# Moving the keys' store and reload from SyncE's queue to GpSimd's, with a new written order of the steps

## The chip, the cores and the metric

The kernel runs on one core of a Trainium2 chip. The metric is the device time of one execution in microseconds; lower is better. Before the change three runs gave a median of 332.5 us (331.88 to 334.31).

## The reference

Two parts follow each other. The first is a linear attention with a complex, data-dependent decay, over 4 batches, 8 heads, 768 tokens and 48 channels per head, all float32:

```python
mag = np.sqrt(a_re * a_re + a_im * a_im)
scale = np.minimum(mag, 0.999) / (mag + 1e-06)
a_re_n, a_im_n = (a_re * scale, a_im * scale)
for t in range(S):
    new_re = ar * S_re - ai * S_im          # ar, ai: a_re_n, a_im_n at token t, per channel d
    new_im = ar * S_im + ai * S_re
    kv = np.einsum('bhd,bhe->bhde', k[:, :, t], v[:, :, t])
    S_re, S_im = (new_re + kv, new_im)
    y[:, :, t] = np.einsum('bhd,bhde->bhe', q[:, :, t], S_re)
```

The second takes y as x, with the heads side by side (4 x 768 x 384), and does a causal convolution over 5 taps per channel, a sigmoid gate and two 384 x 384 products:

```python
for k in range(K):
    gate_pre += conv_w[k][None, None, :] * xp[:, k:k + S, :]
gate = 1.0 / (1.0 + np.exp(-gate_pre))
val = x @ w_val
return (gate * val @ w_out).astype(np.float32)
```

The weights of the second part (w_val, conv_w, w_out) come as 64-bit floats and are turned into 32-bit ones on the chip.

## The kernel before

**Units.** The heads are worked on in 10 units: units 0 and 1 have two heads each, units 2 to 7 four, units 8 and 9 two again. Each unit has 768 tokens, in 6 chunks of 128, and its tokens are split into two halves of 384.

**Preparation of a unit.** The decay's logarithm and angle are summed up along the tokens, so that the recurrence becomes products: a query and a key are each multiplied by a magnitude and by a cosine and a sine, which makes 96 columns per head. The tiles for this have the tokens on partitions in an order of their own (partition p holds three consecutive tokens of each half). The steps: X or x (even or odd units: logarithms and exponentials of the decay, ACT and DVE by turns), R or r (arctangent, sums along the tokens, angle; the offsets between partitions by matmuls), A or a (the magnitude's offsets), S (sine, cosine), E (exponentials), and B, four DVE instructions: the key times its magnitude, then `kx`, the scaled keys with sine and cosine, then the same for the query, into `trig`. Behind the second B letter's instruction two DMAs, one per half of the tokens, store `kx` in a DRAM tile `kd` (line 392).

**Attention of a unit.** T (128 letters): three transpositions on PE turn one half of one head's keys or queries to `kq`, which has the 96 channels on partitions; ACT copies them out of PSUM (line 431). Since the state's update needs keys with the tokens of a chunk on partitions, the keys are read back from `kd` in that layout: N, one letter per half of a unit, sets one column of a `kn` tile to zero on GpSimd (line 407) and issues three DMAs `kn<-kd` (line 413), one for the first half of the heads and two, each with half the rows swapped, for the second. Each waits for its half of the store; the second and third also wait for the first. There are three `kn` tiles. Then by chunk: s (scores on PE), k (mask on DVE), t (state `S_ps` from `kn` and `v`, PE, copied by ACT), y (output from the state and from the masked scores, PE, copied to `y_sb` by ACT). There are two `y_sb` tiles, each for half a unit. D moves such a half into `xT`, channels on partitions, by DMAs issued on GpSimd (`xT<-y_sb`, line 509).

**The second part.** C is the convolution on DVE (lines 518 and 521), G the sigmoid on ACT, M the two products on PE with the gating on DVE and a copy on ACT; O stores the result from GpSimd (line 813). W turns the weights to 32 bits, mostly on DVE (lines 186 to 208), once.

**What sets the order.** Every step is a letter of the string `ORDER` (991 letters); L and V load inputs, issued by SyncE. The instructions of PE, ACT and DVE run in exactly the order of the letters, by dependencies added at the end of the kernel. Those of SyncE and GpSimd are placed by the framework's own scheduler, and each of the two issues its queue in order: a DMA that has to wait keeps all behind it on the same engine from being issued. ACT's function tables are loaded by `table_set` when the next function isn't in the loaded set, so the number of table loads follows from the order.

`XQ` is the name for GpSimd as an issuer of DMAs (`XQ = nc.gpsimd`).

Of the kernel before, what the change touches and what calls it, by code (L numbers as in the profile page):

```python
# [19 lines left out]

PI = math.pi
ORDER = (
    "LLXLXxxXXVxXLxxXXxxXRxrWWWWWLRWWRrrLWLVWRARRALWrarWraARSSWWWaWWWWWrSSEWEBBBLBWXWXEENXLNWTTTWTTWT"
    "XTXTBLsskBXBWkyLWtBTskNXXLtRRxRyWskWWsWxTTxTRykWtRTxWxWxTWWTyLsWkWRtWTxytskxrrDyAttWsksARNSyktSr"
    "DVysWtrAErysWrkWDErBLatBskSatBLyLSkaNByXEWWXyNWTTtDTTTTTTLTWTTTTXTTTtEstBLXsVBktkyXWsBLkWyBskxtX"
    "yDstykWskNXytxWCCCCCTTXTyTTDTTTTxCCTCTTTTVTCTsktCxskCCLCCtNyCxCskCRRCLGMRMMsxtMykMxMyDRAARRsxrrr"
    "ktRSSMMAOMMstrEEOryMrMBLMMrSSBNyaMBLLLOaXMtkXMMaMyMEMDBTTTTTTTTTTTTXTTXTTstEBLMsNtBkykBLxsOMxsNt"
    "yVksXBkXtCysxkXtXyMxMkyxTTTyttTOCTTTTTCTTCTCMDDCOTNxTCTCTCCCCLRCCRCskRstCxCCGMMMMMMRskRtVykLRxrr"
    "rMMORsykAMSyrDMSAAEaOrskrtMrMsOaEBMtLBNykMSyMaMtSEBLLXyBNXMMTTMTTTTTTLTTTTTTTTsEtMXDBLsXBkkBLXLx"
    "txXyskCtysBXMOtCXRRyDskRxkCNtTtTVTTTTTTsxxRAyLRxCkCMANxRxrrAyMMMMOyDtTVTTTTTrTTRSSssCCktCyskCras"  # L30
    "kECtOyCCsEBkrBCCtCCyDBskCtykNCGMaMaMMyMtByMCCCMMOCCCtTDTTTTTTTMsksrtrCNCSMVMCSskMMykOMCMMEEBCOsB"
    "NsBtNMykMMCykMDyMstBTTTTTOTTkTtstykMyDssMtykkMMOtMCCyCsCksCtCCCCCCCOykDCtCCMGCCMstyMMCGMMyMkyMMt"
    "MDMOOMMMMMOCCCCCCGMMMMMMMMOOMMO"
)
IN_ORDER = (
    mybir.EngineType.PE, mybir.EngineType.Activation, mybir.EngineType.DVE
# [9 lines left out]
def kernel(  # L46
# [12 lines left out]
    nc = tc.nc  # L59
    XQ = nc.gpsimd  # L60
# [60 lines left out]
    def rows(h, g):  # L121

        return ((0, 0, C),) if h < g // 2 else ((0, C // 2, C // 2), (C // 2, 0, C // 2))
# [27 lines left out]
    for f in range(2):  # L151
        nc.gpsimd.memset(dmat[:, f], float(f))
        nc.gpsimd.affine_select(
            out=dmat[:, f], in_=dmat[:, f], pattern=[[1, P]], compare_op=ALU.is_ge, fill=float(f - 1),
# [6 lines left out]
    for kind, r0, i0 in ((0, 0, 0), (0, C // 2, C // 2), (1, 0, C // 2), (1, C // 2, 0)):  # L161
        nc.gpsimd.affine_select(
            out=mask[r0:r0 + C // 2, kind], in_=mask[r0:r0 + C // 2, kind], pattern=[[1, C]],
# [100 lines left out]
    def views(u):  # L264
        b, h0, g = units[u]
        main = tiles[u]["main"]
        return main, main.rearrange("p s j f x -> p s (j f x)"), main.rearrange("p s j f (h d) -> p s j (f h) d", h=g)
# [101 lines left out]
    def prep_b(u):  # L369

        b, h0, g = units[u]
        tl = tiles[u]
        trig = tl["trig"]
        main, mf, mj = views(u)

        def scaled(s, nm, dst):
            while not done.get(("L", u, nm)):
                yield "wait"
            nc.vector.tensor_tensor(out=mj[:, s], in0=mj[:, s], in1=jm(tl[nm]), op=ALU.mult)  # L379
            done[nm, u] = True  # L380
            yield
            nc.vector.tensor_tensor(  # L382
                out=dst, in0=trig,
                in1=mj[:, s].rearrange("p j x d -> p (j x) d")[:, :, None, :].to_broadcast([P, J * g, 2, D]),
                op=ALU.mult,
            )
            return dst.rearrange("p (j f h) c d -> p j f h (c d)", f=2, h=g)

        kx = yield from scaled(1, "k", work.tile([P, J * g, 2, D], F32, name="kx", bufs=KXB))
        kd = tl["kd"] = dram.tile([S, g, C2], F32, name="kd")  # L390
        for f in range(2):
            nc.sync.dma_start(
                out=kd[f * HS:(f + 1) * HS].rearrange("(p j) h c -> p j (h c)", j=JH),
                in_=kx[:, :, f].rearrange("p j h c -> p j (h c)"),
            )
        tl["kn"] = []
        done["kd", u] = True
        yield
        qx = yield from scaled(0, "q", trig)
        tl.update(kx=kx, qx=qx, kq=[])  # L400

    def load_kn(u, hn):

        b, h0, g = units[u]
        n0, N = HN * hn, min(HN, NCH - 1 - HN * hn)
        flat = qkp.tile([C, HN * g * C2 + 1], F32, name="kn", bufs=KNB)
        nc.gpsimd.memset(flat[:, N * g * C2:N * g * C2 + 1], 0.0)
        kn = flat[:, :N * g * C2].rearrange("i (n x) -> i n x", n=N)
        src = tiles[u]["kd"][n0 * C:(n0 + N) * C].rearrange("(n i) h c -> i n (h c)", i=C)
        for h in (0, g // 2):  # L410
            cols = slice(h * C2, (h + g // 2) * C2)
            for i0, i1, n in rows(h, g):
                nc.sync.dma_start(out=kn[i0:i0 + n, :, cols], in_=src[i1:i1 + n, :, cols])
        tiles[u]["kn"].append(flat)

    def transpose(u):
# [263 lines left out]
    stream_s = prep_stream("S", prep_s, lambda u: upto("R", u), every)  # L680
    stream_e = prep_stream("E", prep_e, lambda u: upto("A", u) and upto("S", u), every)
    stream_b = prep_stream("B", prep_b, lambda u: upto("E", u) and upto("S", u) and upto("T", u - KXB), every)

    def guard():
# [110 lines left out]
    def move(key):  # L795
# [13 lines left out]
        elif key == "O":  # L809
            if i >= len(outs):  # L810
                return False
            b, m, ot = outs[i]
            XQ.dma_start(out=out[b, m:m + P], in_=ot)
        else:
            if i >= (NU if key == "V" else 2 * NU):
                return False
            u, hn = (i, 0) if key == "V" else halves_of[i]
            if key == "V":
                if u not in tiles or u >= VB and not done.get(("Y", u - VB)):
                    return False  # L820
                load_v(u)
                done["V", u] = True
            elif key == "N":
                if not done.get(("kd", u)) or i >= KNB and at["t"] < HN * (i - KNB + 1) - (i - KNB) % 2:
                    return False
                load_kn(u, hn)
                done["N", u, hn] = True
            else:
                if not done.get(("y", u, HN * hn + HN - 1)) or not room_for_x(units[u][0]):
                    return False  # L830
                att[u].collect(hn)
                done["D", u, hn] = True
# [169 lines left out]
```

## Time and profile before

| | |
|---|---|
| median of three runs | 332.5 us |
| the profiled execution | 332.24 us, of which the span is 330.5 us |
| PE busy | 263.2 us, 80% of the span |
| DVE busy | 257.4 us, 78% |
| ACT busy | 245.9 us, 74% |
| POOL busy | 59.8 us, 18% |
| granted clock of TensorE | 0.94 |
| moved by DMA | 53.31 MB |
| of it by q1 (issued on SyncE) | 43.28 MB |
| of it by q0 (issued on GpSimd) | 9.44 MB |

The profile is of one execution. The span goes from the first to the last instruction; the time of the execution is 1.7 us longer. POOL stands for GpSimd, SPq for SyncE's queue of DMA issues; an issue on GpSimd is shown as an instruction of POOL. A busy PE isn't PE at its peak, since its instructions overlap.

### The profile page before, as it was taken

The page shows a single profiled execution, that of the slowest core. Times are in us where ns is not written, and L with a number is a line of the kernel's source. Part 1 is how long each engine was busy: PE and PEld are TensorE (multiplying, and loading weights), DVE is VectorE, ACT ScalarE, POOL GpSimd, SP SyncE. Part 2 cuts the span into 40 slices and gives each one's busy share as a digit, 9 for nine tenths or more (in the row PEclk, how much of TensorE's full clock was granted, in tenths as well). Part 3 has the DMA queues.
Part 4 walks back from the last instruction along what each step waited for, and adds up shares of the span by engine and source line. Part 5 has one row for each costly group of instructions (what it writes and reads, how often), then busy time and mean ns, then how long its engine had stood idle before and what let it go on. Part 6 is the DMA issues. An engine that isn't in the chain of part 4 may idle for free.

```text
span 330.5 us, 8134 instructions
## 1 busy us (share of the span) xinstructions
PE 263.2 (80%) x3234; PEld 204.1 (62%) x3234; DVE 257.4 (78%) x341; ACT 245.9 (74%) x455; POOL 59.8 (18%) x148
## 2 busy tenths in 40 slices
PE   0030775747999899989969999899998999999950
PEld 0030664635998487668868887698696756866520
DVE  4499889999698999968968999689789857294500
ACT  5729879999979789998849899989894474552110
POOL 3000001121033022030430030303303312132110
PEclk9999959785999799999969999999999999999995
DMA  7994989839999722788989025997424504321120
GB/s 198 279 244 100 264 235 241 173 91 285 237 322 168 195 77 69 236 227 225 278 224 189 3 68 194 246 275 184 122 57 126 137 18 125 84 86 32 60 78 0
DMA packets 87804, 53.31 MB, mean 161 GB/s; under 512 B 36432, under 2 KB 84816, under 8 KB 87760
## 3 DMA queue, kind: packets, MB, share of 16 engines
q1 hardware_dynamic: 83664, 43.28, 50.8%
q0 software_dynamic: 4096, 9.44, 9.4%
q8 instruction: 27, 0.44, 0.6%
q14 instruction: 17, 0.14, 0.1%
HBM read 33.83 MB, written 14.16 MB: 145 GB/s over the span
## 4 chain that ended last, share of the span: by engine, by line
PE 31%; DVE 23%; ACT 14%; issue 12%; DMA 11%; POOL 3%; SPq 2%; POOLq 0%; DVEq 0%; ACTq 0%
PE pt L430 9%; PE pv L255 6%; PE po L255 4%; DMA kn<-kd 4%; ACT L104 3%; PE sc_ps L457 3%; DVE sm L464 3%; PE y_ps L480 3%; DMA raw<-in_moe_w_val_dram 3%; DVE main L379 3%; DMA kd<-kx 3%; DVE main L249 2%; DVE main L318 2%; DMA xT<-y_sb 2%; PE y_ps L477 2%
## 5 line engine op out<-in xcount | busy, mean ns | idle before, releaser
L431 ACT COPY kq<-pt 96x384 f32<-96x384 f32 x128 | 52.0, 508 | 4.7 <-PE pt L430 4.5
L509 POOL DMA_DIRECT2D xT<-y_sb x80 | 41.0, 519 | 77.4 <-ACT y_sb L481 74.9
L521 DVE SCALAR_TENSOR_TENSOR z<-xT,cw_sb,z 128x768 f32<-128x768 f32 (+1 forms) x60 | 51.4, 856 | 1.7
L255 PE MATMUL pv<-xT,wv_sb 128*64 128x384 f32 x288 | 51.4, 499 | 0.0
L255 PE MATMUL po<-wo_sb,z 128*64 128x384 f32 x288 | 51.2, 488 | 0.0
L430 PE MATMUL pt<-ident,kx 128*96 128x128 f32 x192 | 37.2, 308 | 10.4 <-DVE kx L382 9.5
L464 DVE TENSOR_TENSOR sm<-sc_ps,mask 128x512 f32<-128x512 f32 (+1 forms) x60 | 34.6, 578 | 13.0 <-PE sc_ps L458 9.0
L480 PE MATMUL y_ps<-sm,v_in 128*48 128x128 f32 x384 | 41.5, 279 | 3.1 <-DVE sm L464 3.1
L457 PE MATMUL sc_ps<-kq 96*64 96x128 f32 x384 | 42.4, 281 | 1.8 <-DVE sm L464 1.7
L458 PE MATMUL sc_ps<-kq 96*64 96x64 f32 x384 | 42.3, 227 | 0.0
L477 PE MATMUL y_ps<-kq,S_sb 96*48 96x128 f32 x320 | 36.3, 286 | 7.2 <-ACT y_sb L481 4.1
L104 ACT ACT_TABLE_LOAD x31 | 39.8, 1283 | 1.3 <-PEq L986 0.8
L430 PE MATMUL pt<-ident,trig 128*96 128x128 f32 x192 | 36.5, 305 | 4.5 <-DVE trig L382 2.8
L458 PEld LDWEIGHTS sc_ps<-kq 96*64 96x64 f32 x384 | 38.5, 140 | 1.7
L255 PEld LDWEIGHTS pv<-xT,wv_sb 128*64 128x64 f32 x288 | 26.0, 141 | 17.6 <-issue 2.9
L457 PEld LDWEIGHTS sc_ps<-kq 96*64 96x64 f32 x384 | 32.1, 141 | 5.1 <-DVE sm L464 2.6
L255 PEld LDWEIGHTS po<-wo_sb,z 128*64 128x64 f32 x288 | 24.6, 136 | 15.4 <-DVE z L542 1.6
L481 ACT COPY y_sb<-y_ps 112x256 f32<-112x256 f32 (+1 forms) x60 | 19.5, 326 | 19.6 <-PE y_ps L480 19.0
L430 PEld LDWEIGHTS pt<-ident,kx 128*96 128x96 f32 x192 | 23.5, 142 | 15.2 <-issue 11.7
L477 PEld LDWEIGHTS y_ps<-kq,S_sb 96*48 96x48 f32 x320 | 21.3, 125 | 15.1 <-ACT y_sb L481 6.4
L480 PEld LDWEIGHTS y_ps<-sm,v_in 128*48 128x48 f32 x384 | 27.1, 126 | 4.1 <-DVE sm L464 3.9
L494 PE MATMUL S_ps<-v_in,kn 128*64 128x48 f32 x320 | 27.7, 225 | 1.6 <-ACT S_sb L497 1.6
(84 smaller groups left out, 484.5 us busy)
## 6 DMA issues: line engine op xcount, KB each, us to landing
kd<-kx SPq DMA_DIRECT2D x12, 576.0 KB, 5.0
out_dram<-ot POOLq DMA_DIRECT2D x24, 192.0 KB, 2.5
ar_in<-in_a_re_dram SPq DMA_DIRECT2D x12, 288.0 KB, 4.3
ai_in<-in_a_im_dram SPq DMA_DIRECT2D x12, 288.0 KB, 4.7
k_in<-in_k_dram SPq DMA_DIRECT2D x12, 288.0 KB, 4.1
q_in<-in_q_dram SPq DMA_DIRECT2D x12, 288.0 KB, 4.1
xT<-y_sb POOLq DMA_DIRECT2D x48, 72.0 KB, 3.3
v_in<-in_v_dram SPq DMA_DIRECT2D x16, 144.0 KB, 4.9
```

What stands on the lines that cost most here:

```text
L104: nc.scalar.preload_act_table_set(name)
L255: nc.tensor.matmul(out[c:c + 64], lhsT[:, c:c + 64], rhs, **kw)
L430: nc.tensor.transpose(pt[:C2, j, :], src[:, j, f, h, :], ident)
L431: nc.scalar.copy(tj[:, s, f], pt[:C2].rearrange("c j p -> c p j"))
L457: nc.tensor.matmul(sc[lo:lo + half, h, :], k[:, :half], q, start=True, stop=True)
L458: nc.tensor.matmul(sc[hi:hi + half, h, half:], k[:, half:], q[:, half:], start=True, stop=True)
L464: nc.vector.tensor_tensor(out=two(sm), in0=two(sc[:, :g]), in1=mask[:, :, None, :].to_broadcast([C, 2, g // 2, C]), op=ALU.mult)
L477: nc.tensor.matmul(o, self.S_sb[n - 1][:, h * D:(h + 1) * D], self.part(1, h, n), start=True, stop=False)
L480: nc.tensor.matmul(o, vt[:, h, n], sm[:, h, :], start=(n == 0), stop=True)
L494: nc.tensor.matmul(S_all[:64, cols], kn[:, c0:c0 + 64], vt[:, h, n], **at_h)
L509: XQ.dma_start(out=xTs[b][c0 % P:c0 % P + c2 - c0, c0 // P, EXT + hf * HS:EXT + (hf + 1) * HS], in_=self.y[hf][r0:r0 + c2 - c0, h // 2],)
L521: nc.vector.scalar_tensor_tensor(out=z, in0=xT[:, c, EXT + t0 - t:EXT + t0 - t + n], scalar=cw_sb[:, TAPS - 1 - t, c:c + 1], in1=z, op0=AL ...
```

## The change

The two stores `kd<-kx` of a unit and the six loads `kn<-kd` are issued by GpSimd instead of SyncE: 20 and 60 DMAs in all, with the same shapes, sizes and dependencies. `ORDER` is replaced by another string. It has the same length, and every letter occurs in it as often as before. The new order was found by a search whose model lets transfers land later. Nothing else changes.

```diff
--- before.py
+++ after.py
@@ -20,17 +20,17 @@
 
 PI = math.pi
 ORDER = (
-    "LLXLXxxXXVxXLxxXXxxXRxrWWWWWLRWWRrrLWLVWRARRALWrarWraARSSWWWaWWWWWrSSEWEBBBLBWXWXEENXLNWTTTWTTWT"
-    "XTXTBLsskBXBWkyLWtBTskNXXLtRRxRyWskWWsWxTTxTRykWtRTxWxWxTWWTyLsWkWRtWTxytskxrrDyAttWsksARNSyktSr"
-    "DVysWtrAErysWrkWDErBLatBskSatBLyLSkaNByXEWWXyNWTTtDTTTTTTLTWTTTTXTTTtEstBLXsVBktkyXWsBLkWyBskxtX"
-    "yDstykWskNXytxWCCCCCTTXTyTTDTTTTxCCTCTTTTVTCTsktCxskCCLCCtNyCxCskCRRCLGMRMMsxtMykMxMyDRAARRsxrrr"
-    "ktRSSMMAOMMstrEEOryMrMBLMMrSSBNyaMBLLLOaXMtkXMMaMyMEMDBTTTTTTTTTTTTXTTXTTstEBLMsNtBkykBLxsOMxsNt"
-    "yVksXBkXtCysxkXtXyMxMkyxTTTyttTOCTTTTTCTTCTCMDDCOTNxTCTCTCCCCLRCCRCskRstCxCCGMMMMMMRskRtVykLRxrr"
-    "rMMORsykAMSyrDMSAAEaOrskrtMrMsOaEBMtLBNykMSyMaMtSEBLLXyBNXMMTTMTTTTTTLTTTTTTTTsEtMXDBLsXBkkBLXLx"
-    "txXyskCtysBXMOtCXRRyDskRxkCNtTtTVTTTTTTsxxRAyLRxCkCMANxRxrrAyMMMMOyDtTVTTTTTrTTRSSssCCktCyskCras"
-    "kECtOyCCsEBkrBCCtCCyDBskCtykNCGMaMaMMyMtByMCCCMMOCCCtTDTTTTTTTMsksrtrCNCSMVMCSskMMykOMCMMEEBCOsB"
-    "NsBtNMykMMCykMDyMstBTTTTTOTTkTtstykMyDssMtykkMMOtMCCyCsCksCtCCCCCCCOykDCtCCMGCCMstyMMCGMMyMkyMMt"
-    "MDMOOMMMMMOCCCCCCGMMMMMMMMOOMMO"
+    "LLXXXXXLxLXxxXXRRLRLxxxxWWRARxLrRArrWAWrLRSrWrVSaEEBBBrXWXBTWSTaaTWWLSTTTENTLEWWXTNWsskysBLkWBWB"
+    "LksWBtWXXWWWTtykTWxTXWWWWWWtxyskXWxXWVtsyWxWxxWtTtkWWTyxxWTWWWTTskLNsWRWykrRDRtrsrykNsLtyRAtRRVy"
+    "AstkraWkaRSaDyWWskAtrWStyErEWDyVBLBBBLNWLLrSSTETETTTTTTWTTTTTTXTWWTsBsDkNLkWXtBysksXytkstXBBykDL"
+    "stXNykXttxTWTyWCCCCTCXyxTCTXDTTTxTTTTTTCTCTNsktCskCLxCtyCsktLCyxCCCCskRtRRVyskCxGMMMsRMRxRtykMMx"
+    "rrRDySMMOSrAyVAAEErMaDrrBLrMMOaaMMOSBMBLMNSMMELMtXMBNCMMOTTTTTTTTTTTTCTLTCEXTTsBLMstMCCMtMBkysXk"
+    "XtXyBLxCNxsBksytTTXTTTTTTXkytkstDLxxkXytxyTTxTTxTTtTTsOsLxrkyRksDMCCCCstNkRysRrVyDkkRAAtCsRRykAC"
+    "tryCCRSSCCOCCGMMMMryrMaVaEMDrMMEMOBMaLrSSBMMMMBOLBMNTMMTTTCTTTTCTTTCTTLTNEtETXLTssCCkMstkCOysXBL"
+    "tByksMtXBLxkyDkNxMXXBMyXMXMxtTTTxTxTxTXLTxskttyMxrrORMyTTRTTRTTRAtTRRrDTTssMtAAkyraLCskCtRSayCSC"
+    "NstkkaCCyCCOsskDrEEBtryrBVCCCCGMMMyMSMkMMOMMNCCCMtyBOBTTTOTTDTTVTtsCMkstCMOCSMyNMsECCEkstCCMCykM"
+    "ykDsstMMBkBMMMOByCMMNOyMtBMTTtMCCTTTTCTCTtCskytCskytskyskNtDyskOsDCCCCkCCtykCGCMMCyMtCMCMCGyMMMM"
+    "MMDOMMOMMMOCCCCCMCGMMMMMMOMMMOO"
 )
 IN_ORDER = (
     mybir.EngineType.PE, mybir.EngineType.Activation, mybir.EngineType.DVE
@@ -389,7 +389,7 @@
         kx = yield from scaled(1, "k", work.tile([P, J * g, 2, D], F32, name="kx", bufs=KXB))
         kd = tl["kd"] = dram.tile([S, g, C2], F32, name="kd")
         for f in range(2):
-            nc.sync.dma_start(
+            XQ.dma_start(
                 out=kd[f * HS:(f + 1) * HS].rearrange("(p j) h c -> p j (h c)", j=JH),
                 in_=kx[:, :, f].rearrange("p j h c -> p j (h c)"),
             )
@@ -410,7 +410,7 @@
         for h in (0, g // 2):
             cols = slice(h * C2, (h + g // 2) * C2)
             for i0, i1, n in rows(h, g):
-                nc.sync.dma_start(out=kn[i0:i0 + n, :, cols], in_=src[i1:i1 + n, :, cols])
+                XQ.dma_start(out=kn[i0:i0 + n, :, cols], in_=src[i1:i1 + n, :, cols])
         tiles[u]["kn"].append(flat)
 
     def transpose(u):
```

## The prediction

> **What bounds the kernel now.** I read the page's first part, then the busy time by stage, then the waits of each engine, then the chain of waits around the stages in which everything stood still. The page's first part names no single bound:
>
> ```profile
> span 330.5 us, 8134 instructions
> PE 263.2 (80%) x3234; PEld 204.1 (62%) x3234; DVE 257.4 (78%) x341; ACT 245.9 (74%) x455; POOL 59.8 (18%) x148
> ```
>
> Three engines are within 18 us of each other, so the stage decides. Columns below: stage and its length, then busy time of PE, PEld, DVE, ACT, POOL, each with its count, then clock, DMA share, GB/s.
>
> ```profile
> 0.00:20.00 20.00, 0.09 (x2) 0.12 (x4) 10.79 (x20) 11.42 (x17) 3.24 (x23) 1.00 0.91 253
> 20.00:45.00 25.00, 11.93 (x105) 10.17 (x107) 23.29 (x39) 18.92 (x35) 0.11 (x1) 0.94 0.73 187
> 45.00:80.00 35.00, 21.98 (x279) 18.29 (x277) 33.40 (x47) 34.50 (x57) 4.17 (x12) 0.79 0.75 202
> 80.00:318.00 238.00, 228.97 (x2855) 175.51 (x2853) 189.92 (x238) 180.54 (x347) 51.73 (x111) 0.97 0.58 152
> 100.00:120.00 20.00, 18.05 (x217) 13.10 (x219) 18.80 (x22) 16.84 (x31) 2.60 (x6) 0.91 0.78 171
> 160.00:180.00 20.00, 17.14 (x183) 14.71 (x181) 15.73 (x18) 14.82 (x29) 5.22 (x11) 0.83 0.99 225
> 240.00:260.00 20.00, 18.80 (x307) 15.58 (x307) 18.68 (x25) 12.59 (x25) 3.05 (x8) 1.00 0.32 86
> ```
>
> Up to 80 us the preparation of the first units on DVE and ACT bounds the kernel: DVE is idle for 9.2 + 1.7 + 1.6 = 12.5 us there, nearly all of it before 20 us. From 80 to 318 us PE is busy for 229.0 of 238 us. The 9.0 us of PE idle time there are all that better timing alone can bring in this stage; 2.9 of them lie in 160 to 180, where DVE and ACT stand as well, and 1.95 and 1.2 in the other two stages shown.
>
> The stall at 160 to 180 is about the very transfers that the change moves. These are rows of the timeline (start, duration, engine, line):
>
> ```profile
> 148.74 2.56 DVE L382 TENSOR_TENSOR kx<-trig,main 128x2304 f32<-128x2304 f32 x1 [2.91 <-PE pt L430]
> 151.83 1.81 SPq L413 DMA_DIRECT2D kn<-kd  x2
> 153.74 1.46 SPq L132 DMA_DIRECT2D v_in<-in_v_dram  x2
> 155.30 0.66 SPq L392 DMA_DIRECT2D kd<-kx  x1
> 168.97 0.34 PE L495 MATMUL S_ps<-v_in,kn 128*33 128x48 f32 x2 [2.86 <-DMA kn<-kd]
> ```
>
> and of the chain of waits (start, duration):
>
> ```profile
> 155.30 5.14 DMA kd<-kx
> 160.50 4.04 DMA kn<-kd
> 165.25 3.58 DMA kn<-kd
> ```
>
> The scaled keys of unit 5 are done at 151.30, but their store is issued at 155.30: ahead of it on SP stand two loads of unit 4's keys, held until 151.83, and two loads of values. Then store, first load and second load land one after the other (the second load of a half waits for the first), and PE waits 2.86 us at 168.97.
>
> **The change, part by part.** Both orders have the same 991 letters with equal counts of each kind, so the n-th letter of a kind is the same step in both and no arithmetic is added. Three things can change the time: table loads, waits, and what the queues hold up.
>
> *Table loads.* Walking through both strings with the rule of `table_set`, I get 31 loads before, as in the row below, and 29 after.
>
> ```profile
> L104 ACT ACT_TABLE_LOAD x31 | 39.8, 1283 | 1.3 <-PEq L986 0.8
> PE 31%; DVE 23%; ACT 14%; issue 12%; DMA 11%; POOL 3%; SPq 2%; POOLq 0%; DVEq 0%; ACTq 0%
> ```
>
> Two fewer are 2 x 1.283 = 2.57 us of ACT. ACT carries 14% of the chain that ended last, so I count -0.4 us (0 to -2.6).
>
> *The start.* Rows of DVE's groups (mean ns of one), of its timeline, of ACT's copies and of the chain of waits:
>
> ```profile
> L186 DVE TENSOR_SCALAR cvt<-raw 128x384 uint32<-128x384 uint32 x6 | 2.1, 354 | 2.5 <-DMA raw<-in_moe_w_val_dram 2.5
> L191 DVE SCALAR_TENSOR_TENSOR cvt<-raw,cvt 128x384 uint32<-128x384 uint32 x6 | 3.3, 557 | 0.2
> 30.76 1.36 DVE L382 TENSOR_TENSOR kx<-trig,main 128x1152 f32<-128x1152 f32 x1
> 43.98 1.35 DVE L382 TENSOR_TENSOR trig<-trig,main 128x1152 f32<-128x1152 f32 x1
> L431 ACT COPY kq<-pt 96x384 f32<-96x384 f32 x128 | 52.0, 508 | 4.7 <-PE pt L430 4.5
> 77.07 2.47 DVE trig L382
> 79.68 6.70 PE pt L430 x45
> ```
>
> Before unit 0's kx (the second B) the old order has 20 W (weights) letters, the new one 5. Of the 15 between, 11 are DVE instructions of 0.35 to 0.56 us, 5.3 us in sum; two a (1.1 us) come later too. So 6.4 us of DVE work leave the path to that kx, and it should end near 32.12 - 6.4 = 25.7 us; my walk along the ACT and DVE steps of unit 0 gives 25.
>
> But this work is only moved. Up to the 17th T (unit 2's first, at 79.68 us, right behind the DVE row at 77.07) both strings hold exactly the same DVE steps; the new one has three ACT steps of X and E and one of W fewer. That T therefore moves only by what DVE's idle time changes. After unit 0's last B the new string has five W, two a and one X for DVE, 4.8 us, and then the first mask (k), which waits until ACT has copied all eight T of unit 0: eight copies (4.1 us), two table loads (2.6) and S and E of unit 1 between. DVE is idle there for 4 to 5 us. Walked on, unit 1's last B ends at 42.3 us, 3.0 earlier than the 45.3 of before, with 3.6 us more of W and X still to do ahead of unit 2's first T: +0.6 us. The ends are -5 (that wait hidden) and +3 (weights needed before they land). PE starts some 7 us earlier and gains nothing by it, since DVE is the bound until 80 us.
>
> *The waits of the middle.* In the new string the second half of unit 4's key loads (N, letter 436) stands 38 letters ahead of unit 5's kx (letter 474), against two letters before, so the store should not be caught behind them. I take the whole 2.86 us stall as gone: -2.9 (0 to -3.3). The other wait on the path is that of the convolution on y's transfer:
>
> ```profile
> DVE z L518 <- DMA xT<-y_sb: 11.5, 4, 5.1
> SPq L413 <- DMA kn<-kd: 33.6, 17, 4.3
> SPq L413 <- DMA kd<-kx: 22.8, 13, 3.8
> ```
>
> It ends PE idle time in the stages 100 to 120 and 240 to 260, 3.15 us together. Between the last y of a half and the conv that needs it the new string has 3.3 us of DVE work and 10.2 us of PE work for the seventh C letter, where the old one had 2.0 and 5.6, and 5.3 us of DVE work for the 43rd, where it had 1.2. I take two thirds: -2.0 (0 to -3.2).
>
> *The queue.* 20 stores and 60 loads leave SP for POOL, past xT's 80 transfers, the 24 of the output and the memsets.
>
> ```profile
> L413 SPq DMA_DIRECT2D kn<-kd x60: 365/608/1194, 35.4 to 284.4; - x60
> L509 POOL DMA_DIRECT2D xT<-y_sb x80: 497/504/696, 53.3 to 303.8; - x80
> L813 POOL DMA_DIRECT2D out_dram<-ot x24: 542/547/696, 128.8 to 320.3; - x24
> kn<-kd SPq DMA_DIRECT2D x16, 144.0 KB, 3.5
> kn<-kd SPq DMA_DIRECT2D x8, 48.0 KB, 2.4
> xT<-y_sb POOLq DMA_DIRECT2D x16, 48.0 KB, 3.4
> kn<-kd SPq DMA_DIRECT2D x6, 192.0 KB, 4.3
> out_dram<-ot POOLq DMA_DIRECT2D x24, 192.0 KB, 2.5
> ```
>
> At 0.50 to 0.70 us each the 80 add 40 to 56 us to POOL's 59.8, some 108 us in all, far from a bound; SP loses 60 x 0.61 us and more that nobody waits for. How a key transfer lands when POOL issues it, no row shows. At 48 KB POOL's row is 1.0 us above SP's, at 192 KB 1.8 us below; I take +0.9 from the smaller pair, whose sizes are nearer to the 48 to 144 KB of most key loads. Three in line are +2.7 us per half unit (-5.4 to +3.0). Where the order leaves work between kx and the first t this is hidden. It is thinnest in the last unit:
>
> ```profile
> 279.54 5.44 SPq L413 DMA_DIRECT2D kn<-kd  x6
> 288.05 0.27 PE L494 MATMUL S_ps<-v_in,kn 128*64 128x48 f32 x2
> ```
>
> Its six loads are issued by 284.98 and land some 2.4 us later, 0.7 us ahead of its first state; the new string leaves one M letter more and 5 us less PE work of other kinds in between, but only the first half's three loads are needed there. I count +1 (0 to +3).
>
> On this the Trainium skill (DMA: Bandwidth & Descriptors, "Issuing engines are not separate DMA queues") speaks against the change: transfers started from different engines end up on the same DMA engines, and several issuers only save issue time. By it alone the 2.9 us would come from the order, and a move of the queue with the old order would be worth nothing; the late store at 155.30 is a case of an issuer that waits, which the rule leaves room for.
>
> Sum: -0.4 + 0.6 - 2.9 - 2.0 + 1.0 = -3.7. The profiled execution took 332.24 us (span 330.5), so 328.5; the median of the runs, 332.5, lies 0.3 above it, so **328.8 us**.
>
> **The rivals.**
>
> *POOL's queue holds y back (slower).* POOL issues in order. A load of keys that waits there for its store keeps every xT and output transfer behind it from being issued. SP waited 33.6 + 22.8 = 56.4 us in 30 such waits, 17% of the span. Of 20 groups of xT (the D letters) 3.4 would fall into such a wait and lose 1.9 us (the mean) to 4.3 us (the longest): 6.5 to 14.6 us, of which the convolutions and, through y's two buffers, ACT take most, since xT waits were on the path before any of this. With the xT gain gone and the rest kept (-1.7) this is 337 to 345, likeliest 339. It decides once an xT issue starts over about 3.3 us (the DVE work left) after its y copy. Against it: POOL is 18% busy, and nothing in the order of SP and POOL is fixed by hand.
>
> *PE takes it all back (no change).* 229.0 of 238 us are busy on PE, so a wait that goes at one place comes back at the next T burst, where ACT's copies set the pace, and 331 to 334 remains, likeliest 332. For it: at the start an earlier PE buys nothing either. Here too belongs that the move does not do what it says, because a load held on POOL is held as long as on SP.
>
> *The start pays (clearly faster).* If DVE finds work during the wait for unit 0's copies, its idle time falls from 12.5 to about 7.5 us and everything behind follows: 328.8 - 5.6 = 323. Against it: the letters there are k, s and y, which all need the copies.
>
> **How the numbers follow.** A difference of about 1% (3.3 us) is what a measurement of this kernel can tell from no change. My forecast, 325 to 331, has 0.38; the start that pays 0.13; no change 0.24; POOL's hold 0.25. Of the forecast 0.30 lies under 329.2, so faster is 0.30 + 0.13 = 0.43, same 0.08 + 0.24 = 0.32, slower 0.25. Cases of both signs are likely, so the range has to reach to both: 320 to 340 leaves out about a tenth at either end; the likeliest case's own range is 325 to 331.
>
> **What would show it.** Right: 29 table loads; q1's bytes down and q0's up by what kd and kn hold; POOL near 108 us; the first kx near 25 us but unit 2's first T still at 78 to 83 us; no wait of PE on kn over 2 us in mid-kernel; DVE's wait on xT under 8 us. Wrong: xT issues on POOL that start more than 3 us after their y copy with a key load in front; long waits of ACT's y copy; unit 2's first T earlier than 76 us; PE's idle time from 80 us on above 9 us.

## The result, and the profile after

The changed kernel takes **343.3 us** (median; 342.6 to 344.6) against 333.1 us of the kernel before on the same chip: recorded ratio 1.0355, 95% interval 1.0315 to 1.0396 (the quotient of the two medians is 1.030). It is 10 us slower; the prediction was 328.8 us, range 320 to 340. A run more than 1.5% above the fastest of its kernel counts as slow and is left out of all medians and ratios here, which among the experiments concerns one run each of e3 and e4.

Page of the changed kernel (busy time by engine; the two queues; shares of the chain that ended last; the table loads):

```profile
span 342.0 us, 8080 instructions
PE 267.9 (78%) x3234; PEld 199.4 (58%) x3234; DVE 259.9 (76%) x341; ACT 242.2 (71%) x453; POOL 113.9 (33%) x228
...
q1 hardware_dynamic: 61904, 25.98, 31.1%
q0 software_dynamic: 9568, 26.75, 26.3%
...
DVE 29%; DMA 20%; ACT 16%; PE 14%; issue 12%; POOL 5%; SPq 0%; POOLq 0%; DVEq 0%; ACTq 0%
...
L104 ACT ACT_TABLE_LOAD x29 | 37.2, 1283 | 1.3 <-PEq L986 0.8
```

PE, DVE and ACT do the work they did before, within 5 us each, in a span that is 11.5 us longer. What grew is the DMA's share of the chain that ended last: 20%, against 11% before. Busy time by stage, with the columns of the prediction's table (the last two are the DMA engines' share and GB/s):

```profile
20.00:45.00 25.00, 12.33 (x102) 9.71 (x99) 19.04 (x31) 17.18 (x31) 7.82 (x11) 0.82 1.00 249
45.00:80.00 35.00, 20.57 (x260) 16.62 (x260) 34.34 (x49) 29.98 (x55) 9.38 (x22) 0.79 0.51 115
80.00:329.00 249.00, 231.28 (x2848) 170.84 (x2849) 194.88 (x241) 178.89 (x347) 92.39 (x171) 0.97 0.55 149
100.00:120.00 20.00, 14.04 (x173) 11.51 (x169) 15.14 (x18) 13.05 (x29) 8.06 (x16) 0.86 1.08 231
```

Two places stand out. From 20 to 45 us DVE is idle for 6.0 us (1.7 before), and from 100 to 120 us PE is idle for 6.0 us (1.95 before). The chain of waits runs through DMAs in both:

```profile
24.64 2.94 DMA kd<-kx
27.86 6.26 DMA kn<-kd
35.04 7.01 DMA kn<-kd
...
99.05 6.69 DMA kn<-kd
...
108.56 7.07 DMA xT<-y_sb
```

The start: `kx` of unit 0 ends at 24.3 us, 7.8 us earlier than before, and then three landings follow in line, 16.2 us together. The last of them ends at 42.04, where unit 0's first key tile is whole, and only then PE can go on. These are rows of SyncE's timeline for that time, and of GpSimd's for that time and for the second place:

```profile
26.82 1.05 SPq L114 DMA_DIRECT2D k_in<-in_k_dram  x2
27.96 1.00 SPq L114 DMA_DIRECT2D q_in<-in_q_dram  x2
...
36.57 1.80 SPq L114 DMA_DIRECT2D q_in<-in_q_dram  x2
```

```profile
34.41 2.42 POOL L413 DMA_DIRECT2D kn<-kd  x4 [4.45 <-DMA kn<-kd]
...
106.03 1.97 POOL L413 DMA_DIRECT2D kn<-kd  x3 [3.70 <-DMA kn<-kd]
...
108.03 2.54 POOL L509 DMA_DIRECT2D xT<-y_sb  x5
```

SyncE, which has no key loads any more, issues input loads from 26.8 to 38.4 us without a stop. The keys issued by GpSimd share the DMA engines with them: the DMA engines' share from 20 to 45 us is 1.00, against 0.73 before. The waits of the changed kernel (us in total, times, longest):

```profile
POOL kn L413 <- DMA kn<-kd: 30.4, 15, 4.8
POOL kn L413 <- DMA kd<-kx: 28.2, 15, 5.6
PE S_ps L495 <- DMA kn<-kd: 11.3, 3, 7.3
DVE z L518 <- DMA xT<-y_sb: 9.1, 4, 4.6
```

GpSimd now does the waiting that SyncE did (58.6 us; SyncE 56.4), and PE's longest wait on keys is 7.3 us.

### The profile page after: what moved, and what is told of

Its sections match the earlier page's. It is cut to its first block, busy times and chain, and to the rows that moved or that the text cites. A ratio compares the mean times of both kernels' runs of the same rounds, so it can differ in the third digit from the quotient of the medians.

```text
span 342.0 us, 8080 instructions
## 1 busy us (share of the span) xinstructions
PE 267.9 (78%) x3234; PEld 199.4 (58%) x3234; DVE 259.9 (76%) x341; ACT 242.2 (71%) x453; POOL 113.9 (33%) x228
## 4 chain that ended last, share of the span: by engine, by line
DVE 29%; DMA 20%; ACT 16%; PE 14%; issue 12%; POOL 5%; SPq 0%; POOLq 0%; DVEq 0%; ACTq 0%
DMA kn<-kd 11%; DVE z L521 5%; PE po L255 5%; DMA xT<-y_sb 4%; PE pt L430 4%; DVE kx L382 4%; DMA kd<-kx 3%; DVE main L379 3%; ACT L104 3%; ACT kq L431 3%; DVE sm L464 3%; DVE main L249 2%; DVE main L318 2%; PE pv L255 2%; POOL xT L509 2%
## 5 line engine op out<-in xcount | busy, mean ns | idle before, releaser
L413 POOL DMA_DIRECT2D kn<-kd x60 | 39.4, 659 | 59.0 <-DMA kn<-kd 30.4
L255 PE MATMUL pv<-xT,wv_sb 128*64 128x384 f32 x288 | 49.7, 486 | 0.0
L457 PE MATMUL sc_ps<-kq 96*64 96x128 f32 x384 | 44.1, 286 | 5.4 <-DVE sm L464 3.4
L430 PE MATMUL pt<-ident,kx 128*96 128x128 f32 x192 | 35.8, 300 | 10.1 <-DVE kx L382 9.7
L430 PE MATMUL pt<-ident,trig 128*96 128x128 f32 x192 | 35.2, 296 | 7.8 <-DVE trig L382 3.1
L497 ACT COPY S_sb<-S_ps 96x192 f32<-96x192 f32 (+1 forms) x50 | 14.4, 287 | 35.9 <-PE S_ps L495 25.1
L477 PE MATMUL y_ps<-kq,S_sb 96*48 96x128 f32 x320 | 35.6, 284 | 2.6 <-ACT y_sb L481 2.3
L255 PEld LDWEIGHTS po<-wo_sb,z 128*64 128x64 f32 x288 | 22.3, 138 | 22.4 <-issue 11.7
L255 PEld LDWEIGHTS pv<-xT,wv_sb 128*64 128x64 f32 x288 | 23.8, 137 | 18.0 <-issue 7.3
L495 PE MATMUL S_ps<-v_in,kn 128*33 128x48 f32 x320 | 24.4, 216 | 11.4 <-DMA kn<-kd 11.3
L430 PEld LDWEIGHTS pt<-ident,kx 128*96 128x96 f32 x192 | 22.6, 138 | 14.7 <-issue 12.0
```

The source lines that it names most:

```text
L255: nc.tensor.matmul(out[c:c + 64], lhsT[:, c:c + 64], rhs, **kw)
L413: XQ.dma_start(out=kn[i0:i0 + n, :, cols], in_=src[i1:i1 + n, :, cols])
L430: nc.tensor.transpose(pt[:C2, j, :], src[:, j, f, h, :], ident)
L457: nc.tensor.matmul(sc[lo:lo + half, h, :], k[:, :half], q, start=True, stop=True)
L477: nc.tensor.matmul(o, self.S_sb[n - 1][:, h * D:(h + 1) * D], self.part(1, h, n), start=True, stop=False)
```

## The experiments

One thing about the end of the program has to be known first: from the issue of the last output to the end of the span 5.1 to 10.2 us pass, depending on which queues GpSimd serves. So the table gives, beside each median, this **end** as each kernel's own profile shows it, and the median **less the end**, which is what the body of the work takes. Each ratio is the recorded one, to runs of the kernel before on the same chip, and can differ by up to 0.009 from the quotient of the medians. The medians of the kernel before were 331.0 to 333.1 us from chip to chip, and the end is that of a single execution. Differences of less than some 3 us in the last column therefore show nothing.

| kernel | median us | ratio to before (95%) | end | less the end |
|---|---|---|---|---|
| before | 332.5 | | 10.2 | 322.3 |
| changed | 343.3 | 1.036 (1.032 to 1.040) | 9.5 | 333.7 |
| e1 old order, keys on GpSimd | 360.8 | 1.082 (1.075 to 1.089) | 9.7 | 351.1 |
| e2 new order, keys on SyncE | 332.4 | 0.999 (0.996 to 1.002) | 10.2 | 322.2 |
| e3 changed, store on SyncE | 346.3 | 1.032 (1.024 to 1.041) | 5.8 | 340.5 |
| e4 changed, y on SyncE | 339.0 | 1.014 (1.008 to 1.020) | 5.6 | 333.4 |
| e5 queues' roles exchanged | 335.4 | 1.012 (1.003 to 1.020) | 6.1 | 329.3 |
| e6 changed, keys in halves | 337.3 | 1.017 (1.009 to 1.026) | 9.5 | 327.8 |
| e7 as e2, keys in halves | 333.8 | 1.007 (1.003 to 1.011) | 10.2 | 323.6 |
| e9 as e6, y on SyncE | 333.2 | 1.007 (1.002 to 1.011) | 5.6 | 327.6 |
| e10 as e5, first loads on SyncE | 327.6 | 0.983 (0.976 to 0.989) | 6.1 | 321.5 |
| e11 before, keys in halves | 332.3 | 0.995 (0.992 to 0.999) | 10.2 | 322.1 |
| e12 before, last outputs on SyncE | 326.6 | 0.981 (0.977 to 0.986) | 5.7 | 320.9 |
| e13 as e2, last outputs on SyncE | 327.3 | 0.985 (0.981 to 0.988) | 6.1 | 321.2 |
| e14 changed, inputs on GpSimd too | 332.7 | 1.001 (0.997 to 1.004) | 5.1 | 327.6 |

**e1 and e2: the two halves of the change, each alone.** e1 is the changed kernel with the old `ORDER`, e2 with the new one and

```diff
-            XQ.dma_start(          # kd<-kx, and the same for kn<-kd
+            nc.sync.dma_start(
```

> The old order, with the store and the loads of the keys issued by GpSimd: the queue's part of the change alone. If the queue costs the time (key loads waiting on GpSimd hold y's transfers, and SyncE, freed of its waits, lets input loads run ahead into the same DMA engines): 339 to 346 us, loads of the keys landing in over 4.5 us in the median of the 288 KB ones and PE waiting over 8 us for them in all. If the new order costs it: 331 to 336 us.

> The new order, with store and loads of the keys still issued by SyncE: the order's part alone. If the queue costs the time: 328 to 334 us, unit 0's loads landing in 3 to 4 us each and PE not waiting for them near 42 us. If the order costs it (keys and inputs asked for too close together at the start, too little work between): 340 us or more, and PE waits over 5 us near 42 us here too.

Measured: 360.8 and 332.4 us; e1 lies 15 us above its expected range. The new order by itself is worth nothing; the queue by itself costs 28.8 us with the old order (less the end), and 11.5 us are left of it with the new one. So the new order does what it was searched for, it bears late transfers better, but it only softens a loss that the move brings in. Waits of e1:

```profile
POOL kn L413 <- DMA kd<-kx: 33.0, 16, 5.9
DVE z L518 <- DMA xT<-y_sb: 16.6, 4, 5.0
PE S_ps L495 <- DMA kn<-kd: 16.3, 4, 5.0
```

And SyncE's timeline in e2, at the start:

```profile
26.62 1.25 SPq L392 DMA_DIRECT2D kd<-kx  x2
27.97 0.57 SPq L114 DMA_DIRECT2D q_in<-in_q_dram  x1
30.38 0.38 SPq L413 DMA_DIRECT2D kn<-kd  x1
30.81 0.48 SPq L114 DMA_DIRECT2D q_in<-in_q_dram  x1
31.38 0.46 SPq L413 DMA_DIRECT2D kn<-kd  x1
31.93 0.54 SPq L114 DMA_DIRECT2D ar_in<-in_a_re_dram  x1
33.62 2.58 SPq L413 DMA_DIRECT2D kn<-kd  x4
```

The store goes out 2.4 us late here, and still the first key tile is whole at 36.74, 5.3 us earlier than in the changed kernel. Between 27 and 36 us SyncE lets out three input loads, and nine in the changed kernel: the second and the third (30.81 and 31.93) come only behind a key load that had to wait for the store.

**e3 and e4: one of GpSimd's jobs given back.** The changed kernel with the store (line 392), or y's transfers (line 509), on `nc.sync`.

> As after the change, but the store of the keys stays on SyncE and only the 60 loads are on GpSimd. If waits on GpSimd for the first loads' landing hold y back, nothing is changed by it: 341 to 345 us. If SyncE's running ahead is the cause, a store that waits on SyncE for kx holds the input loads back again: 334 to 339 us, with unit 0's loads landing faster than 6 us.

> As after the change, but y's transfers into xT are issued by SyncE, so that no key load can stand in front of them. If GpSimd's queue holding y back is the main cost: 333 to 338 us, and DVE waits under 4 us for xT. If the cost is the late landing of the keys beside the input loads: 340 to 345 us, with PE still waiting 7 us near 42 us.

Measured: 346.3 and 339.0 us. e3 misses both of its ranges: the store stands behind input loads on SyncE (unit 0's goes out 4.0 us after `kx`), and the body is slower still, by 7 us by the medians and by 3 by the ratios. With y on SyncE the median falls by 4.3, but 3.9 of it are the end (9.5 to 5.6 us): the body stays, as closely as these few runs tell. (The profiled execution of e4 took 342.1 us, above its median; only the end is read from it.) The expectation of e9 below still takes this gain for y's freedom.

**e5 and e10: the roles of the queues exchanged.** Against e2, every input load, the store and the key loads are issued by GpSimd, y's transfers and the output by SyncE. e10 leaves the first four input loads on SyncE.

```diff
-    def load(u, nm):                       # e5: IQ = nc.gpsimd for all loads
-            nc.sync.dma_start(
+    def load(u, nm, IQ=IQ):                # e10: load(0, "ar", nc.sync) and three more
+            IQ.dma_start(
...
-                    XQ.dma_start(          # xT<-y_sb, and the same for out
+                    nc.sync.dma_start(
```

> The new order with the two queues' roles exchanged against the kernel with the new order and the keys on SyncE (328.4 us span, 332.4 median): every input load, the key stores and the key loads are issued by GpSimd, and only y's transfers and the output by SyncE. The input loads so stand again in one line with the waits of the keys, but the line is GpSimd's. Theory A (loads that run ahead on a free SyncE share the DMA engines with the key loads): unit 0's key loads land 3 to 4 us after their issue as they did from SyncE (3.2 and 2.8 to 3.1), no wait of PE on kn is over 3 us, and the time is 330 to 336. Theory B (a key load issued by GpSimd is slow by itself): unit 0's key loads take 6 to 7 us as in the changed kernel, PE waits 10 us or more on kn in sum, and the time is 340 or more.

> The kernel with the two queues' roles exchanged, but its first four input loads issued by SyncE again, since on GpSimd their 5.8 us of issue stood ahead of the constants and made unit 0's first kx end at 30.4 us, not 24.3. Theory A (a key load from GpSimd costs no more than one from SyncE, as long as the input loads stand in line with the keys' waits): the profiled span is 328 to 330 us and the median 331 to 333.5, as with the keys on SyncE (328.4 and 332.4). Theory B (some price of GpSimd's issue remains): 335 or more.

e5's first `kx` ends at 30.4 us, since 5.8 us of issue stand ahead of GpSimd's constants; with that gone e10 takes 327.6 us, 321.5 less the end: as good as e2 from SyncE, and some 12 us better than the changed kernel, though the keys are on GpSimd in both and each first load still holds back the two behind it. Waits in e10:

```profile
DVE z L518 <- DMA xT<-y_sb: 4.8, 3, 2.5
PE S_ps L495 <- DMA kn<-kd: 2.2, 2, 1.2
```

So a key load issued by GpSimd isn't slow by itself. It has what e2 had: the inputs in line with the keys' waits, and y on the other queue, alone with the output.

**e6 and e7: the line of landings made shorter.** In the key tile, each half of the heads becomes one contiguous stretch, so the second and third load don't wait for the first.

```diff
-        kn = flat[:, :N * g * C2].rearrange("i (n x) -> i n x", n=N)
+        m = g // 2
+        kn = flat[:, :N * g * C2].rearrange("i (f n x) -> i f n x", f=2, n=N)
...
-                XQ.dma_start(out=kn[i0:i0 + n, :, cols], in_=src[i1:i1 + n, :, cols])
+                XQ.dma_start(out=kn[i0:i0 + n, h // m], in_=src[i1:i1 + n, :, cols])
...
-                c0 = (n % HN * self.g + h) * C2
+                m, N = self.g // 2, min(HN, NCH - 1 - HN * (n // HN))
+                c0 = ((h // m * N + n % HN) * m + h % m) * C2
```

> The changed kernel, with the key tile laid out so that each half of the heads is one contiguous stretch: the second and third load of a tile then need not wait for the first to land, and the three go out together behind their store. Queues and order stay. Theory A (the price of the change is the line of landings: store, first load, the other two): unit 0's last key load lands at 36 to 38 us, not 42, PE's waits on kn fall from 11.3 us to under 5, and the time falls by 5 to 10 us to 333 to 338. Theory C (the price is y's transfers held behind the waits of the keys on GpSimd): those waits on the store (28.2 us) stay, DVE's wait on xT stays near 9 us, and the time stays at 340 to 343.

> The new order with the keys on SyncE and the same layout of the key tile in two contiguous halves of heads, so that a tile's three loads go out together. Theory A (the line of landings is on the path with SyncE as well): unit 0's last load lands near 34 us, not 36.7, the waits of PE on kn vanish, and the time falls from 332.4 to 326 to 330. Rival (PE and DVE take it back, as they took back the gains of the new order): 331 to 333.

e6 takes 337.3 us, 5.9 less than the changed kernel in the body; e7 gains nothing over e2. Waits of e6, and its key loads of 144 KB (count, size, median us to landing):

```profile
DVE z L520 <- DMA xT<-y_sb: 9.2, 5, 4.5
PE S_ps L496 <- DMA kn<-kd: 0.5, 1, 0.5
```

```profile
kn<-kd POOLq DMA_DIRECT2D x16, 144.0 KB, 5.9
```

In the changed kernel:

```profile
kn<-kd POOLq DMA_DIRECT2D x16, 144.0 KB, 3.8
```

PE's waits on keys are gone, although each load, three at a time, now lands later. DVE's waits on y are what they were, and half of the loss stays: against e2, `kx` shows 5.3 us lost between units 3 and 4, where DVE waits 4.5 us for y.

**e8: a shorter backlog.** The changed kernel without the load of w_out (`raws.append(raws[0])` in its place).

> The changed kernel without the load of w_out: both weight tiles are made from w_val, so the projection's second matrix is the wrong one and 1.2 MB of input are not moved at the start. All else stays. Theory A (the key loads land late because other loads share the DMA engines): with the engines' backlog shorter by some 6 us at the start, unit 0's first key load lands 3 to 4.5 us after its issue, not 6.3, and the other two 3 to 4.5, not 5.6 and 7.0; the time is 338 to 341. Theory B (slow by itself): 6 to 7 us as before, and the time stays at 342 to 344.

Unit 0's key loads landed 3.8, 4.3 and 4.5 us after their issue, as theory A had it. But its store took 5.1 us, not 2.9, presumably because the input loads behind the missing one moved up and met it there; the time was 342.1 us (one run), which theory B had. So the landings depend on the traffic, but a backlog that is only shifted isn't worth time.

**e9 and e11: the repairs combined, and the old order with keys in halves.** e9 is e6 with line 509's transfers on `nc.sync`; e11 is the kernel before with e7's layout.

> The changed kernel with both single repairs together: the key tile in two contiguous halves of heads (alone: 337.3 us) and y's transfers issued by SyncE (alone: 339.3 us); the keys stay on GpSimd, the order is the new one. Theory D (the 10 us of the queue's move are two separate prices, the line of the key landings and y's transfers held behind waiting key loads): the gains add, 343.3 - 6.0 - 4.0 = 333.3 us (331 to 335), PE waits under 1 us on kn and DVE's wait on xT falls below 5 us. Rival (both repairs win back the same time): 336 to 338.

> The kernel before, with its old order and its keys on SyncE, and only the key tile laid out in two contiguous halves of heads. The stall of 2.86 us that the prediction counted off, and PE's waits on kn (4.9 us the longest), should be gone. If waits that leave the path turn into time: 328 to 330. Rival (PE and DVE take it back, as they did with the new order on SyncE): 331.5 to 333.5.

e9's 333.2 us is what theory D said, but that is chance, and the theory is wrong: 3.9 of the 4.1 us against e6 are the end, and the body stays (327.6 and 327.8). On SyncE y stands behind input loads instead; DVE waits there for 4.8 us at 111 us. e11 gains 0.5% at most, but doesn't test what its expectation asks: the stall stayed. PE still waits 2.48 us for keys at 169.5 us (2.86 before), so what its going would be worth there is not shown.

**e12 and e13: the end alone.** In the kernel before, and in e2, the last image's six outputs go to SyncE:

```diff
-            XQ.dma_start(out=out[b, m:m + P], in_=ot)
+            (nc.sync if b == B - 1 else XQ).dma_start(out=out[b, m:m + P], in_=ot)
```

> The kernel before, unchanged but for the last image's six output transfers, which SyncE issues. In the profile of before, GpSimd closes with a DRAIN of 8.56 us (321.09 to 329.65) that starts behind its last output's issue, and the span ends 7.7 us after the last output has landed (322.75); in the kernel with the roles exchanged, where SyncE issues the outputs, the end comes 1.7 us after the last landing. Theory E (what was gained there is this DRAIN, which starts earlier and is hidden when GpSimd is done earlier): the DRAIN starts near 305 us and ends before 316, the span ends some 2 us after the last output's landing, at 324.5 to 326, and the median is 326 to 328. Rival (the gain was in the exchanged roles of the queues, and the closing takes its time whatever issues the outputs): 331.5 to 334.

> The new order with the keys on SyncE, and the last image's six output transfers issued by SyncE too. Its last output landed at 320.85 us, 1.9 us earlier than in the kernel before, and 7.5 us went by from there to the end. Theory E: span 322.5 to 324.5, median 324 to 326.5, so it is below the old order with the same change by about 2 us. Rival (as above): 331 to 334.

326.6 and 327.3 us: ratio 0.981 (0.977 to 0.986) for e12, the fastest kernel here, by one line. The rows of the program's closing line (ns min/median/max of the instructions; start of the first and the last), of before and of e12:

```profile
L997 POOLq DRAIN  x3: 40/107/8559, 321.1 to 330.2; - x3
```

```profile
L997 POOLq DRAIN  x3: 40/107/8069, 305.0 to 324.7; - x3
```

GpSimd's DRAIN of 8 us is still there, but it starts at 305.0 us, behind the last y transfer, and is over while PE is still at work. e13 isn't below e12: once more the new order is worth nothing.

**e14: only the inputs moved into the keys' queue.** e10 with y and the output back on GpSimd, so that it is the changed kernel with nothing but the input loads moved.

> The new order with every transfer on GpSimd (inputs, keys, y and the output) but the first four input loads: the kernel with the exchanged roles, with y's transfers and the output put back behind the keys. It is the changed kernel with nothing but the input loads moved, into the queue of the keys. GpSimd closes the program again, so some 7 us from the last landing to the end are to be taken off before it is compared. Theory A (the price of the change is that input loads, no longer in line with the keys' waits, run ahead and share the DMA engines with the keys): without the closing 325.5 to 328.5 us, a median of 332.5 to 335.5, although the keys' waits stand in front of y on GpSimd. Theory C (y must not stand behind the keys' waits): the waits of DVE on xT come back to 9 us or more and the time without the closing is 331 or more, a median of 338 or more.

332.7 us, no slower than before. Part of that is the end (5.1 us, its DRAIN 3.4). Less the end it is 327.6: 6.1 us of the 11.4 are back. Counted from the last landing, as the expectation did, it is 330.3, between the two theories; C's mark, waits of DVE on xT of 9 us, isn't met: 4.6, or 7.0 with the wait at 180.65 below, which the profile puts down to `kn`. GpSimd's timeline at the start, and busy time from 26 to 40 us, of e14 and then of the changed kernel:

```profile
24.91 1.47 POOL L392 DMA_DIRECT2D kd<-kx  x2 [0.63 <-DVE kx L382]
26.15 1.00 POOL L114 DMA_DIRECT2D k_in<-in_k_dram  x1
26.91 0.98 POOL L114 DMA_DIRECT2D q_in<-in_q_dram  x1
28.73 0.74 POOL L413 DMA_DIRECT2D kn<-kd  x1 [0.84 <-DMA kd<-kx]
29.47 0.77 POOL L114 DMA_DIRECT2D q_in<-in_q_dram  x1
30.23 0.71 POOL L413 DMA_DIRECT2D kn<-kd  x1
```

```profile
26.00:40.00 14.00, 9.80 (x106) 8.22 (x108) 13.08 (x23) 12.61 (x27) 11.91 (x18) 1.00 0.82 233
```

```profile
26.00:40.00 14.00, 7.61 (x59) 6.50 (x59) 12.66 (x23) 8.98 (x19) 5.70 (x9) 0.85 1.10 278
```

With the inputs in line the DMA engines' share falls from 1.10 to 0.82 in these 14 us, the first key load lands 3.5 us after its issue (6.3 in the changed kernel), and unit 0's first key tile is whole at 35.6 us, not 42.0. At the same time y is held longer than in the changed kernel (up to 9.2 us behind its copy, against 2.8). The other 6.1 us come when y and the output leave this queue (e10).

The ends of `kx` tell where the time goes. Against e2 the changed kernel loses 5.3 us up to unit 2, 4.8 between units 3 and 4 and 4.0 between units 5 and 6. e14 loses 1.4, 0.5 and 5.4 there, e10 0.5, 0.1 and 1.4. So the inputs in line repair the first two places, and the third gets worse. There, in e14, y copied at 172.57 stands behind an output and three input loads:

```profile
172.50 0.58 POOL L813 DMA_DIRECT2D out_dram<-ot  x1
175.50 2.54 POOL L509 DMA_DIRECT2D xT<-y_sb  x5
...
180.65 0.77 DVE L518 TENSOR_SCALAR z<-xT,cw_sb 128x768 f32<-128x768 f32 x1 [2.42 <-DMA kn<-kd]
...
185.24 0.47 PE L457 MATMUL sc_ps<-kq 96*64 96x128 f32 x1 [4.03 <-DVE sm L464]
```

(The convolution reads `xT` and not `kn`; the name in the brackets is inferred.) In the changed kernel no convolution waits between these two `kx`; PE waits 1.97 us for keys at 164.6.

So of the 11.4 us some 6 at least are the price of inputs that run ahead of the keys; e14 shows it by itself. The rest comes back when y and the output leave a queue on which other transfers wait, but only if the inputs aren't on their new queue (e10 against e14; e4 and e9 gained nothing in the body). This second step is measured on e14, where y is held longest. In the changed kernel y's part may be smaller and that of the inputs larger: no run gives y a queue of its own while inputs and keys are apart. e2 and e10, where neither happens, have the same body whichever engine has which role. Two things stay open: how the 11.4 us divide between inputs and y, and how much of the inputs' price is the sharing of the DMA engines and how much the line of landings (e6 wins 5.9 us by shortening it).

## Why the prediction was wrong, point by point

**The queue** is the step that failed. The prediction had "SP loses 60 x 0.61 us and more that nobody waits for" and +1 (0 to +3) for the landings. SyncE's 56.4 us of waiting were not idle: they held the input loads back while keys were on their way. With the waits gone the inputs ran ahead, and the term was +11.4 with the new order, some 6 of it at least by the inputs (e14), and +28.8 with the old. The prediction's own sign of this, PE idle for more than 9 us from 80 us on, came out at 17.7 us.

**The bounds of a landing** were taken from pairs of rows by size and queue (+0.9, from -1.8), as if the issuer made the difference. In e10 GpSimd issues the keys and their medians are as from SyncE in e2 (48 KB: 2.3 and 2.4 us, 144 KB: 4.1 and 3.8). In the changed kernel they rose unevenly (192 KB: 4.3 before and after; 288 KB: 3.6 to 4.9), and unloaded loads land alike (unit 8's first: 2.6 us, 2.3 in e2). What moved were those that meet input loads: 19 of the 60 took over 5 us, 3 before, and on the path they took 6.3, 7.0 and 6.7 us. A median over 16 transfers doesn't show the price of the three on the path.

**The place.** The prediction looked for the thinnest cover in the last unit. Against e2, `kx` of the changed kernel ends 5.3 us later in unit 2, 10.2 in unit 4, 14.2 in unit 6 and 14.2 in unit 9: the losses are at unit 0, between units 3 and 4 and between units 5 and 6, and none at the end.

**The order's terms**, -2.9 for the stall and -2.0 for xT, came to 0: e2's waits of PE on keys fell to 2.1 us and DVE's on xT to 4.4, as foreseen, and the time stayed (0.999, 0.996 to 1.002). "PE takes it all back" was right for the order, and e13 says the same; where PE spends the time that it no longer waits is not shown. The 29 **table loads** were right and can't be seen in the time.

**The start.** The first `kx` came at 24.3 us (foreseen near 25). Unit 2's `kx` ended at 73.8 in e2 against 73.4, so the +0.6 was right for the order; the changed kernel has 79.1. One reading was wrong: the row at 79.68 is unit 2's first query. Its first T, of a key, starts at 77.05 before, at 73.99 in e2 and at 79.24 after the change.

**The rival "POOL's queue holds y back"** had the direction, a quarter of the chance and 337 to 345 us, with the measured 343.3 inside. How far its mechanism holds is open. Its own sign isn't met: y's issue came at most 2.8 us after its copy, under the 3.3 us from which it was to decide. But those 2.8 us stand where it counts. The five transfers at 108.03 come behind key loads that had waited 3.70 us, and DVE's longest wait for them (4.6 us, at 115.75) is made of this hold and of landings of up to 7 us. e4 and e9 can't part the two, since on SyncE input loads held y instead (in e9 4.1 us at the same place).

**The rule of the Trainium skill** quoted there (DMA: Bandwidth & Descriptors, "Issuing engines are not separate DMA queues") was read as "a move of the queue with the old order would be worth nothing". e1 measured +28.8 us. That the queues share the DMA engines agrees with the trace (share 1.10 from 26 to 40 us); what follows for a move is another thing, since here each queue is issued in order by itself and a second one takes away what held the first back.

## What to carry to other kernels

A wait on an in-order DMA queue is also a brake on what stands behind it: before moving the waiting transfers away, ask what the freed queue will send, and when. Keep bulk prefetches in line with the urgent transfers that should go first, and give transfers that must go at once a queue on which nothing waits; here such an arrangement took as long with either engine in either role (e2 and e10). Look at the end of the program separately, since an edit that moves a queue can change it by 4 us and pass for a gain in the body.

## What the runs showed that I had not expected

GpSimd's closing DRAIN lasts 8.56 us where it issues y and the output, 8.1 without the last six outputs, 7.6 to 7.8 with all the keys as well, and 3.4 to 4.0 where the store or y is taken from it or the inputs are added; it is hidden when GpSimd's last transfer comes some 15 us before the last output. It doesn't follow the number of transfers (e4 and the kernel before have 104 each, with 3.99 and 8.56 us), and what sets its length stays open.

New and old order differ by 17 us when transfers land late (e1 against the changed kernel) and by nothing when they don't (e2).
